# Another order of units in a fused attention and FFN kernel on one core

## The chip, the core and the metric

The kernel runs on one core of a Trainium2 chip. Its matrix engine (TensorE, PE in the profile; PEld are its weight loads), VectorE (DVE), ScalarE (ACT), GpSimd (POOL) and the queue engine SyncE (SP), which here issues the transfers, each take their own instructions strictly in program order and wait for one another by semaphores. The metric is the device time of one execution in microseconds (us), the median of several runs. The profile's span of one execution is a little shorter than that time.

## What is computed

Attention with a local window of 96 keys and 8 global keys, for 4 batches of 8 heads, 768 positions and 64 channels, followed by a feed-forward layer with a maximum of three products:

```
scores = q @ k.T / 8 - slope[head] * dist          # masked to (0 <= i - j < 96) or (j < 8)
a      = softmax(scores)
x      = concat_heads(a @ v)                       # 3072 tokens x 512
h      = max(x @ w1, x @ w2, x @ w3)               # 512 -> 768
out    = h @ w_out                                 # 768 -> 512, float32
```

Inputs and output are float32; the kernel multiplies in bfloat16 and accumulates in float32. The window lets each tile of 128 tokens attend only to itself and the tile before it, whose first 8 key columns and v rows are overwritten with the global ones.

## The kernel before

The program is a list of small units. A string names them in order, and each engine gets its instructions in that order. A unit is a letter, then indices, then often a digit that chooses the engine (0 ScalarE, 1 VectorE, 2 GpSimd; 3 and 4 other ways). The start of the string and the places that the change touches most (cuts marked):

```
SCHEDULE = """
    K0 K1 K2 K3 K4 K5 l1.0 l1.1 D0.3 c0.0.2 B0.1 B1.1 B2.1 B3.0 K6 B4.1 B5.1 c0.1.1 c1.0.2 x0.0.4 B6.1
    B7.1 x0.1.4 S0.0.1 v0 l2.0 l2.1 K7 S0.1.1 G0.0 S1.0.1 S1.1.0 x1.0.3 c1.1.2 M0.0 M0.1 M1.0 v1 x1.1.4
    C0.1.2 v2 A0.1 G1.2 S2.0.1 M1.1 c2.0.2 x2.0.1 C1.1.1 S2.1.0 G2.2 S3.0.1 M2.0 M2.1 C2.1.1 T0.1 S3.1.1
    M3.0 M3.1 c2.1.2 v3 A1.0 C3.1.0 w0.0 V1.2 x2.1.2 w1.0 A2.1 V2.2 A3.0 T1.0 T2.1 T3.1 W1.0.1 W0.0.0
    G3.2 S4.0.0 S4.1.0 F0.0.0 F0.1.0 M4.0 F0.2.0 F0.3.0 G4.1 S5.0.0 M4.1 S5.1.0 w0.1 W0.1.1 w0.2 W0.2.2
    ...
    F6.2.1 F6.1.2 F6.3.1 F6.4.1 F6.2.2 F6.3.2 F6.5.0 F6.4.2 F6.5.1 F6.5.2 E
"""
```

The letters: `l`, `L` load q and k (`l` several tiles at once), `v` loads v, `w` and `o` load weights; `c`, `C`, `W`, `Q` cast what was loaded to bfloat16; `x`, `X` transpose q and k; `K`, `B` make the masks; `S` scores and their exp, `M` the mask, `A` the product with v and the division, `T` the transpose of its result, `G`, `V` copy the global rows; `F c.f.j` is the product of FFN chunk c, 128 columns f, with weight j, `O` the output product of one tile, `E` the last ones, `D` matmuls of zeros. A chunk is 4, 2, 2, 4, 4, 4, 4 tiles in turn. The first six tiles are read by `l` in pairs, then tiles 6 to 9 and 10, 11; later tiles one by one. PSUM has 3 slots for `psH`, one for `psT` and two for scores.

The units of which the prediction speaks, at the lines of the profile (L239 x, L261 X, L283 and L275 S, L288 its exp, L307 M, L322 and L325 A, L349 T, L361 F, L376 O, L427 W, L436 D):

```python
def u_x(n, s, how):
    bb, t0, sz, a, j0, jn = part(n, s)
    dst = batch_T(bb)[:, a, j0:j0 + jn, t0 * 128:(t0 + sz) * 128].rearrange("c j (i e) -> c j i e", e=sz)
    if how >= 4 and jn > 1:
        m = jn // 2
        halves = [(0, m, psT, "tp", nc.scalar.copy), (m, jn, psH, "h", nc.vector.tensor_copy)]
    else:
        pool, tag = (psH, "h") if how in (2, 3) else (psT, "tp")
        halves = [(0, jn, pool, tag, copies[how % 2])]
    tps = [pool.tile([128, sz, hi - lo, 128], BF16, name="tpp", tag=tag) for lo, hi, pool, tag, copy in halves]
    for (lo, hi, pool, tag, copy), tp in zip(halves, tps):
        for e in range(sz):
            for j in range(lo, hi):
                nc.tensor.transpose(tp[:, e, j - lo],
                                    qb["p", n, s][:, e, 2 * j:2 * j + 2].rearrange("i h d -> i (h d)"), identb)
    for (lo, hi, pool, tag, copy), tp in zip(halves, tps):
        copy(dst[:, lo:hi], tp.rearrange("c e j i -> c j i e"))

def u_X(T, how):
    pt = batch_T(T // NT)
    t = T % NT
    qk = pt[:, :, :, 128 * t:128 * t + 128]
    if how == 4:
        nc.sync.dma_start_transpose(out=qk.rearrange("p a j s -> p (a j) s"),
                                    in_=qb[T].rearrange("p a c -> p (a c)"))
        return
    if how == 3:
        tps = [psT.tile([128, NP, 128], BF16, name="tp", tag="tp"),
               psH.tile([128, NP, 128], BF16, name="tpk", tag="h")]
    else:
        tp = psT.tile([128, 2, NP, 128], BF16, name="tp", tag="tp")
        tps = [tp[:, a] for a in range(2)]
    for a in range(2):
        for jp in range(NP):
            nc.tensor.transpose(tps[a][:, jp], qb[T][:, a, jp * 128:(jp + 1) * 128], identb)
    if how == 3:
        nc.scalar.copy(qk[:, 0], tps[0])
        nc.vector.tensor_copy(qk[:, 1], tps[1])
    else:
        copies[how](qk, tp)

def u_S(T, g, how):
    b, t = divmod(T, NT)
    sp = psS.tile([128, 2, 2, 2, 128], FP32, name="sp", tag=f"sp{g}")
    n = 2 if t else 1
    if how:
        for hh in range(2):
            nc.tensor.matmul(sp[:, hh, :, 0:n], identb,
                             bias[:, g, hh, :, 0:2] if t else bias[:, g, hh, :, 2:3],
                             start=True, stop=False, skip_group_check=True)
    for ds in range(2 if t else 1):
        for j2 in range(2):
            jp = 2 * g + j2
            for hh in range(2):
                hsl = slice(64 * hh, 64 * hh + 64)
                nc.tensor.matmul(sp[:, hh, j2, ds], qT(T - ds, 1)[hsl, jp], qT(T, 0)[hsl, jp],
                                 start=not how, stop=True, skip_group_check=True)
    P = p_pool.tile([128, 4, 2, 128], BF16, name="P", tag="P")
    Pt[T, g] = P
    masked[T, g] = how
    nc.scalar.activation(P[:, :, 0:n], sp.rearrange("p a b d n -> p (a b) d n")[:, :, 0:n],
                         AF.Exp, bias=0.0, scale=scale)

def u_A(T, how):
    b, t = divmod(T, NT)
    op = psS.tile([128, 2, 512], FP32, name="op", tag=f"sp{how}")
    for g in range(2):
        P = Pt[T, g]
        for j2 in range(2):
            for hh in range(2):
                h = 4 * g + 2 * j2 + hh
                i = 2 * hh + j2
                o = op[:, g, (2 * j2 + hh) * 65:(2 * j2 + hh) * 65 + 65]
                nc.tensor.matmul(o, P[:, i, 0], heads(va[T])[:, h], start=True, stop=(t == 0),
                                 skip_group_check=True)
                if t:
                    nc.tensor.matmul(o, P[:, i, 1], heads(va[T - 1])[:, h], start=False, stop=True,
                                     skip_group_check=True)
    x = xb_pool.tile([128, H, D], BF16, name="xb", tag="xb")
    xb[T] = x
    rz = z_pool.tile([128, 2, 4], FP32, name="rz", tag="rz")
    o4 = op[:, :, 0:260].rearrange("p g (h e) -> p g h e", e=65)
    nc.vector.reciprocal(rz, o4[:, :, :, 64])
    nc.vector.tensor_tensor(out=x.rearrange("p (g h) d -> p g h d", g=2), in0=o4[:, :, :, 0:64],
                            in1=rz[:, :, :, None].to_broadcast([128, 2, 4, D]), op=ALU.mult)

def u_XT(T, how):
    c, i = where[T]
    if i == 0:
        xT[c] = xT_pool.tile([128, NP, len(chunks[c]) * 128], BF16, name="xT", tag="xT")
    if how == 4:
        nc.sync.dma_start_transpose(out=xT[c][:, :, i * 128:(i + 1) * 128],
                                    in_=xb[T].rearrange("p h d -> p (h d)"))
        return
    if early(T):
        tp = psH.tile([128, NP, 128], BF16, name="xtp", tag="h")
    else:
        tp = psT.tile([128, NP, 128], BF16, name="xtp", tag="tp")
    x = xb[T].rearrange("p h d -> p (h d)")
    for jp in range(NP):
        nc.tensor.transpose(tp[:, jp], x[:, jp * 128:(jp + 1) * 128], identb)
    copies[how](xT[c][:, :, i * 128:(i + 1) * 128], tp)

def u_F1(c, f, j):
    W = len(chunks[c]) * 128
    if f == 0 and j == 0:
        ht[c] = ht_pool.tile([128, NF, W], BF16, name="ht", tag="ht")
    ps = psH.tile([128, W], FP32, name="h", tag="h")
    for dm in range(4):
        nc.tensor.matmul(ps, w123[f // 2][:, dm, j, (f % 2) * 128:(f % 2) * 128 + 128],
                         xT[c][:, dm], start=(dm == 0), stop=(dm == 3))
    if j == 0:
        h01 = h01_pool.tile([128, W], BF16, name="h01", tag="h01")
        h01s[c, f] = h01
        nc.scalar.copy(h01, ps)
    elif j == 1:
        nc.vector.tensor_max(h01s[c, f], h01s[c, f], ps)
    else:
        nc.vector.tensor_max(ht[c][:, f], h01s[c, f], ps)

def u_E():
    n = len(chunks[last])
    pos = [psH.tile([128, DM], FP32, name="po", tag="h") for _ in range(2)]
    for tt in range(2):
        f2_mm(pos[tt], last, tt, range(NF - 1))
    for tt in range(2):
        f2_mm(pos[tt], last, tt, [NF - 1])
        f2_out(pos[tt], last, tt, nc.scalar.copy)
    for tt in range(2, n - 1):
        po = psT.tile([128, DM], FP32, name="po", tag="tp")
        f2_mm(po, last, tt, range(NF))
        f2_out(po, last, tt, nc.scalar.copy)
    for lo, hi, copy, dma in ((0, 256, nc.scalar.copy, nc.sync), (256, 384, nc.vector.tensor_copy, nc.sync),
                              (384, 512, nc.scalar.copy, nc.scalar)):
        po = psH.tile([128, hi - lo], FP32, name="po", tag="h")
        f2_mm(po, last, n - 1, range(NF), slice(lo, hi))
        f2_out(po, last, n - 1, copy, slice(lo, hi), dma)

def u_D(i, n):
    wp = psH.tile([128, 512], FP32, name="wp", tag="h")
    for _ in range(n):
        nc.tensor.matmul(wp, zeros[:, 0:128], zeros, start=True, stop=True)
```

Of the kernel before, what the change touches and what calls it, by code (L numbers as in the profile page):

```python
# [25 lines left out]
    K0 K1 K2 K3 K4 K5 l1.0 l1.1 D0.3 c0.0.2 B0.1 B1.1 B2.1 B3.0 K6 B4.1 B5.1 c0.1.1 c1.0.2 x0.0.4 B6.1  # L26
    B7.1 x0.1.4 S0.0.1 v0 l2.0 l2.1 K7 S0.1.1 G0.0 S1.0.1 S1.1.0 x1.0.3 c1.1.2 M0.0 M0.1 M1.0 v1 x1.1.4
    C0.1.2 v2 A0.1 G1.2 S2.0.1 M1.1 c2.0.2 x2.0.1 C1.1.1 S2.1.0 G2.2 S3.0.1 M2.0 M2.1 C2.1.1 T0.1 S3.1.1
    M3.0 M3.1 c2.1.2 v3 A1.0 C3.1.0 w0.0 V1.2 x2.1.2 w1.0 A2.1 V2.2 A3.0 T1.0 T2.1 T3.1 W1.0.1 W0.0.0
    G3.2 S4.0.0 S4.1.0 F0.0.0 F0.1.0 M4.0 F0.2.0 F0.3.0 G4.1 S5.0.0 M4.1 S5.1.0 w0.1 W0.1.1 w0.2 W0.2.2  # L30
    V3.2 F0.0.1 F0.1.1 F0.0.2 F0.1.2 v4 C4.1.0 A4.0 V4.2 w1.1 W1.1.2 W2.0.0 F0.4.0 F0.5.0 M5.0 M5.1 w1.2
    W1.2.2 v5 W2.1.0 T4.0 F0.2.1 F0.3.1 l3.0 l3.2 F0.4.1 l3.1 c3.0.2 c3.2.2 F0.5.1 o2 C5.1.0 A5.1 l3.3
    F0.2.2 Q2.2 F0.3.2 W2.2.0 o0 T5.0 F0.4.2 o1 F0.5.2 x3.0.0 F1.0.0 F1.1.0 c3.1.1 F1.2.0 x3.2.0 Q0.2
    F1.0.1 F1.1.1 F1.2.1 l4.0 l4.1 c3.3.0 F1.0.2 F1.1.2 F1.2.2 x3.1.2 x3.3.1 F1.3.0 F1.4.0 Q1.2 F1.3.1
    S6.0.0 S6.1.0 v6 v7 v8 G6.0 F1.3.2 F1.5.0 v9 c4.0.1 F1.4.1 S7.0.0 S7.1.0 G7.2 v10 M6.0 M6.1 M7.0
    M7.1 O0.0.0 F1.4.2 c4.1.1 C6.1.2 C7.1.2 L12 F1.5.1 S8.0.0 S8.1.0 x4.0.0 O0.1.0 A6.0 x4.1.2 A7.1 V7.2
    F1.5.2 v11 T6.0 O0.2.0 T7.1 G8.2 C8.1.2 S9.0.0 S9.1.0 G9.1 v12 v13 O0.3.0 F2.0.0 F2.1.0 S10.0.0 M8.0
# [23 lines left out]
def kernel(  # L61
# [13 lines left out]
    nc = tc.nc  # L75
# [46 lines left out]
    zeros = persist.tile([128, 512], BF16, name="zeros")  # L122
# [387 lines left out]
```

The softmax here doesn't subtract the row's maximum and nothing guards it: scores larger than these inputs give would overflow.

## Time and profile before

| what | value |
|---|---|
| time, median of 3 | 180.43 us (180.39 to 180.48) |
| span of the profiled execution | 178.5 us |
| h matmuls (L361), records | 491, busy 99.2 us |
| output matmuls (L376), records | 147, busy 33.1 us |
| transposes by DMA | 11 of x, 9 of q and k |
| HBM traffic | 25.17 MB read, 6.29 MB written |

A busy time is the union of the intervals in which an engine worked; shares are of the span. The chain that ended last is followed back from the last instruction to whatever released each step; its rows give start, length and what ran. A few per cent of the matmul records are missing from the trace, so counts of the program are larger. PEclk is the share of the clock that was granted.

### The profile page before, as it was taken

The page shows a single profiled execution, that of the slowest core. Times are in us where ns is not written, and L with a number is a line of the kernel's source. Part 1 is how long each engine was busy: PE and PEld are TensorE (multiplying, and loading weights), DVE is VectorE, ACT ScalarE, POOL GpSimd, SP SyncE. Part 2 cuts the span into 40 slices and gives each one's busy share as a digit, 9 for nine tenths or more (in the row PEclk, how much of TensorE's full clock was granted, in tenths as well). Part 3 has the DMA queues.
Part 4 walks back from the last instruction along what each step waited for, and adds up shares of the span by engine and source line. Part 5 has one row for each costly group of instructions (what it writes and reads, how often), then busy time and mean ns, then how long its engine had stood idle before and what let it go on. Part 6 is the DMA issues. An engine that isn't in the chain of part 4 may idle for free.

```text
span 178.5 us, 3963 instructions
## 1 busy us (share of the span) xinstructions
PE 167.1 (94%) x1529; PEld 95.9 (54%) x1551; DVE 119.1 (67%) x237; ACT 103.2 (58%) x160; POOL 37.4 (21%) x65
## 2 busy tenths in 40 slices
PE   3599799999999999999999999999999999999991
PEld 0455645458866677845555555454454555444451
DVE  4519975977796689748978448978358986137610
ACT  4867898646689958555753936351862543440131
POOL 4255203543343012210006024100020401000000
PEclk9999999999999999999999999999999999999998
DMA  5999999999998899899544999988989664700015
GB/s 139 292 270 243 357 321 383 319 361 356 252 194 229 218 254 227 142 204 234 92 90 122 167 253 231 145 172 152 182 156 300 123 129 147 252 12 4 0 47 190
DMA packets 83587, 35.52 MB, mean 199 GB/s; under 512 B 66160, under 2 KB 78320, under 8 KB 83568
## 3 DMA queue, kind: packets, MB, share of 16 engines
q1 hardware_dynamic: 83424, 35.20, 83.6%
q8 instruction: 12, 0.20, 0.5%
q10 hardware_dynamic: 144, 0.07, 0.1%
q14 instruction: 7, 0.06, 0.1%
HBM read 25.17 MB, written 6.29 MB: 176 GB/s over the span
## 4 chain that ended last, share of the span: by engine, by line
PE 88%; ACT 3%; DVE 2%; POOL 2%; issue 1%; DMA 1%; POOLq 0%; ACTq 0%
PE h L361 53%; PE po L376 16%; PE sp L283 7%; PE op L322 3%; PE op L325 3%; PE tpp L239 3%; PE xtp L349 2%; ACT wmask L300 2%; PE sp L275 2%; DMA out_dram<-ost 1%; DVE qkT L243 1%; DVE xb L332 1%; ACT ost L382 1%; ACT P L288 1%; PE tp L261 1%
## 5 line engine op out<-in xcount | busy, mean ns | idle before, releaser
L361 PE MATMUL h<-xT,w 128*128 128x512 bf16 (+1 forms) x491 | 99.2, 348 | 0.7 <-issue 0.2
L361 PEld LDWEIGHTS <-w 128*128 128x128 bf16 x504 | 47.0, 98 | 40.4 <-ACT w L427 0.2
L288 ACT ACTIVATE P<-sp 128x1024 bf16<-128x1024 f32 (+1 forms) x48 | 43.4, 954 | 20.4 <-PE sp L283 20.2
L368 DVE TENSOR_TENSOR h<-h,h 128x512 bf16<-128x512 bf16 (+1 forms) x42 | 25.2, 609 | 25.6 <-PE h L361 15.5
L366 ACT CAST h<-h 128x512 bf16<-128x512 f32 (+1 forms) x42 | 21.6, 532 | 21.5 <-PE h L361 21.3
L376 PE MATMUL po<-wo,ht 128*128 128x512 bf16 (+2 forms) x147 | 33.1, 362 | 0.5
L370 DVE TENSOR_TENSOR ht<-h,h 128x512 bf16<-128x512 bf16 (+1 forms) x42 | 25.0, 606 | 3.7 <-PE h L361 3.0
L307 DVE TENSOR_TENSOR P<-P,wmask 128x1024 bf16<-128x1024 bf16 x36 | 24.8, 716 | 3.6 <-ACT P L288 3.5
L382 ACT COPY ost<-po 128x512 f32<-128x512 f32 (+2 forms) x20 | 11.2, 564 | 18.4 <-PE po L376 11.2
L376 PEld LDWEIGHTS <-ht 128*128 128x128 bf16 x156 | 14.0, 98 | 13.8
L332 DVE TENSOR_TENSOR xb<-op,rz 128x512 bf16<-128x512 f32 x24 | 16.6, 691 | 0.8
L283 PEld LDWEIGHTS <-qkT 64*128 64x128 bf16 x352 | 10.2, 96 | 10.0 <-issue 8.0
L283 PE MATMUL sp<-qkT 64*128 64x128 bf16 x352 | 15.2, 223 | 0.4 <-DVE xb L332 0.4
L322 PEld LDWEIGHTS <-P 128*128 128x128 bf16 x192 | 12.5, 97 | 2.7 <-ACT P L288 0.2
L221 POOL COPY va<-vaf 8x260 int32<-8x260 int32 x14 | 6.3, 449 | 34.7 <-PE op L325 34.7
L198 POOL CAST qkb<-raw 128x1024 bf16<-128x1024 f32 x7 | 7.2, 1037 | 27.6 <-DMA raw<-in_k_dram 27.6
L322 PE MATMUL op<-va,P 128*128 128x65 bf16 x160 | 12.4, 193 | 0.3 <-ACT va L189 0.2
L239 PE MATMUL tpp<-identb,qkp 128*128 128x128 bf16 x96 | 8.5, 246 | 4.0 <-POOL qkp L183 3.5
L325 PEld LDWEIGHTS <-P 128*128 128x128 bf16 x160 | 10.4, 97 | 1.8 <-issue 0.2
L239 PEld LDWEIGHTS <-qkp 128*128 128x128 bf16 x96 | 7.0, 112 | 5.8 <-POOL qkp L183 4.4
L325 PE MATMUL op<-va,P 128*128 128x65 bf16 x128 | 9.9, 193 | 0.1
L243 ACT COPY qkT<-tpp 128x1024 bf16<-128x1024 bf16 (+1 forms) x9 | 7.9, 873 | 3.4 <-PE tpp L239 3.4
(66 smaller groups left out, 107.7 us busy)
## 6 DMA issues: line engine op xcount, KB each, us to landing
rawv<-in_v_dram SPq DMA_DIRECT2D x24, 256.0 KB, 4.9
out_dram<-ost SPq DMA_DIRECT2D x23, 256.0 KB, 2.3
rawp<-in_q_dram SPq DMA_DIRECT2D x6, 512.0 KB, 7.3
rawp<-in_k_dram SPq DMA_DIRECT2D x6, 512.0 KB, 7.7
wst<-in_moe_w_dram SPq DMA_DIRECT2D x3, 1024.0 KB, 10.3
raw<-in_q_dram SPq DMA_DIRECT2D x12, 256.0 KB, 4.2
raw<-in_k_dram SPq DMA_DIRECT2D x12, 256.0 KB, 4.7
wst<-in_moe_w_dram SPq DMA_DIRECT2D x3, 512.0 KB, 8.6
```

The costliest lines, as they stand in the source:

```text
L239: nc.tensor.transpose(tp[:, e, j - lo], qb["p", n, s][:, e, 2 * j:2 * j + 2].rearrange("i h d -> i (h d)"), identb)
L283: nc.tensor.matmul(sp[:, hh, j2, ds], qT(T - ds, 1)[hsl, jp], qT(T, 0)[hsl, jp], start=not how, stop=True, skip_group_check=True)
L288: nc.scalar.activation(P[:, :, 0:n], sp.rearrange("p a b d n -> p (a b) d n")[:, :, 0:n], AF.Exp, bias=0.0, scale=scale)
L307: nc.vector.tensor_mul(P, P, wmask[:, g, :, 0:2])
L322: nc.tensor.matmul(o, P[:, i, 0], heads(va[T])[:, h], start=True, stop=(t == 0), skip_group_check=True)
L325: nc.tensor.matmul(o, P[:, i, 1], heads(va[T - 1])[:, h], start=False, stop=True, skip_group_check=True)
L332: nc.vector.tensor_tensor(out=x.rearrange("p (g h) d -> p g h d", g=2), in0=o4[:, :, :, 0:64], in1=rz[:, :, :, None].to_broadcast([128, 2, ...
L361: nc.tensor.matmul(ps, w123[f // 2][:, dm, j, (f % 2) * 128:(f % 2) * 128 + 128], xT[c][:, dm], start=(dm == 0), stop=(dm == 3))
L366: nc.scalar.copy(h01, ps)
L368: nc.vector.tensor_max(h01s[c, f], h01s[c, f], ps)
L370: nc.vector.tensor_max(ht[c][:, f], h01s[c, f], ps)
L376: nc.tensor.matmul(po, ht[c][:, f, tt * 128:(tt + 1) * 128], wo[:, f, cols], start=(f == 0), stop=(f == NF - 1))
```

## The change

The whole list is put into another order. v of tiles 1 and 2 is loaded ahead of the third pair's q and k, and the three first weight blocks w0.0, w0.1, w0.2 ahead of the larger w1.0. The masks that are needed later are made later. The unit of zeros has 54 matmuls of 128 columns instead of 3 of 512; they keep TensorE at work from the start until the first data are there. The transposes of x for tiles 6 to 9 and of q and k for tiles 12, 16 and 18 go from TensorE to DMA, which takes work from TensorE and copies from VectorE and ScalarE. Many casts and small copies move to another engine. A unit of 9 short matmuls of zeros stands after the last unit. What is computed stays the same.

The diff, cut to the head, the places of the moved transposes and the end:

```diff
 SCHEDULE = """
-    K0 K1 K2 K3 K4 K5 l1.0 l1.1 D0.3 c0.0.2 B0.1 B1.1 B2.1 B3.0 K6 B4.1 B5.1 c0.1.1 c1.0.2 x0.0.4 B6.1
-    B7.1 x0.1.4 S0.0.1 v0 l2.0 l2.1 K7 S0.1.1 G0.0 S1.0.1 S1.1.0 x1.0.3 c1.1.2 M0.0 M0.1 M1.0 v1 x1.1.4
-    C0.1.2 v2 A0.1 G1.2 S2.0.1 M1.1 c2.0.2 x2.0.1 C1.1.1 S2.1.0 G2.2 S3.0.1 M2.0 M2.1 C2.1.1 T0.1 S3.1.1
-    M3.0 M3.1 c2.1.2 v3 A1.0 C3.1.0 w0.0 V1.2 x2.1.2 w1.0 A2.1 V2.2 A3.0 T1.0 T2.1 T3.1 W1.0.1 W0.0.0
-    G3.2 S4.0.0 S4.1.0 F0.0.0 F0.1.0 M4.0 F0.2.0 F0.3.0 G4.1 S5.0.0 M4.1 S5.1.0 w0.1 W0.1.1 w0.2 W0.2.2
-    V3.2 F0.0.1 F0.1.1 F0.0.2 F0.1.2 v4 C4.1.0 A4.0 V4.2 w1.1 W1.1.2 W2.0.0 F0.4.0 F0.5.0 M5.0 M5.1 w1.2
-    ... (cut)
-    F1.5.2 v11 T6.0 O0.2.0 T7.1 G8.2 C8.1.2 S9.0.0 S9.1.0 G9.1 v12 v13 O0.3.0 F2.0.0 F2.1.0 S10.0.0 M8.0
-    ... (cut)
-    A9.1 X12.1 M10.0 M10.1 C10.1.0 C11.1.0 F2.2.0 S11.0.0 S11.1.0 M11.0 M11.1 L15 F2.3.0 F2.4.0 O1.1.0
-    V9.2 A10.1 F2.2.1 V10.2 T8.0 F2.3.1 F2.5.0 T9.0 A11.1 F2.4.1 T10.0 F2.2.2 F2.3.2 T11.1 F2.4.2
-    ... (cut)
-    V14.2 F3.3.2 F3.4.2 T13.4 F3.5.2 C16.1.0 C16.0.2 X16.3 T14.4 C17.0.2 A15.1 X17.4 O2.1.0 S16.0.0
-    ... (cut)
-    A16.1 F4.2.0 F4.3.0 S17.0.0 S17.1.0 F4.2.1 F4.0.2 F4.3.1 v18 M17.0 v19 M17.1 X18.3 X19.4 C20.0.0
-    ... (cut)
-    A23.1 T23.4 O5.0.1 O5.1.0 O5.2.1 O5.3.0 F6.0.0 F6.1.0 F6.0.1 F6.0.2 F6.2.0 F6.3.0 F6.4.0 F6.1.1
-    F6.2.1 F6.1.2 F6.3.1 F6.4.1 F6.2.2 F6.3.2 F6.5.0 F6.4.2 F6.5.1 F6.5.2 E
+    B6.1 K5 B5.1 D0.54 l1.0 K6 c1.0.2 B4.1 B0.1 B2.1 K0 B3.0 B7.1 B1.1 c0.1.1 c0.0.0 x0.0.3 K4 x0.1.4 K7
+    S0.1.1 S0.0.1 l1.1 c1.1.1 G0.0 S1.1.0 v0 C0.1.1 S1.0.1 G1.1 x1.0.3 M0.1 M0.0 x1.1.4 A0.1 M1.0 v1 v2
+    S2.0.1 S2.1.0 G2.2 M1.1 S3.0.1 S3.1.1 C1.1.1 C2.1.2 M2.0 M2.1 l2.1 c2.1.1 A1.0 V1.2 K1 x2.1.4 v3
+    T0.1 C3.1.2 A2.1 V2.0 l2.0 c2.0.0 G3.0 w0.0 T1.0 A3.0 x2.0.4 M3.0 w0.1 T2.0 T3.1 w0.2 W0.0.2 W0.2.1
+    W0.1.2 S4.0.0 S4.1.0 M4.1 G4.0 F0.0.0 F0.1.0 F0.1.1 K2 F0.0.1 S5.0.0 S5.1.0 V3.2 w1.0 W1.0.1 F0.0.2
+    K3 M5.0 F0.1.2 F0.3.0 M4.0 F0.2.0 w1.1 W1.1.1 W2.0.2 F0.5.0 F0.4.0 W2.1.2 F0.5.1 v4 C4.1.2 A4.0
+    F0.4.1 M5.1 F0.3.1 w1.2 W2.2.0 W1.2.2 T4.1 V4.2 F0.2.1 M3.1 F0.5.2 v5 C5.1.0 A5.0 l3.1 c3.1.2 F0.3.2
+    F0.2.2 T5.1 l3.0 c3.0.0 x3.1.3 F0.4.2 F1.0.0 F1.4.0 x3.0.4 F1.0.1 F1.0.2 l3.2 c3.2.2 x3.2.3 l3.3
+    ... (cut)
+    v9 Q1.2 G8.1 l4.0 F1.3.2 M7.1 F1.5.1 F1.5.2 O0.2.0 M8.1 A6.1 T6.4 v10 A7.0 V7.2 T7.4 F1.4.2 L12 M8.0
+    O0.0.0 S9.1.0 S9.0.0 c4.1.2 x4.1.4 O0.3.0 M9.1 c4.0.2 M9.0 L13 O0.1.0 L14 x4.0.4 C8.1.2 A8.1 F2.0.0
+    F2.1.0 C11.1.0 F2.3.0 C10.1.1 T8.4 G9.2 S10.0.0 S10.1.0 C9.1.2 F2.1.1 V8.1 F2.0.1 F2.1.2 A9.0 V9.2
+    ... (cut)
+    F2.2.1 V10.0 T9.4 F2.5.0 A11.1 F2.4.0 C13.0.2 X13.4 F2.2.2 T10.1 v13 X12.4 F2.5.1 G12.2 C14.0.2
+    ... (cut)
+    C18.1.2 T13.4 F3.5.1 T14.4 F3.5.2 C16.0.0 S15.1.0 M15.1 S15.0.0 X16.4 X18.4 G15.1 V14.1 L19 O3.2.1
+    ... (cut)
+    O5.0.0 O4.3.0 O5.2.0 F6.0.0 F6.4.0 F6.4.1 O5.3.1 F6.2.0 F6.2.1 O5.1.1 F6.2.2 F6.4.2 F6.0.1 F6.0.2
+    F6.3.0 F6.3.1 F6.3.2 F6.5.0 F6.1.0 F6.1.1 F6.1.2 F6.5.1 F6.5.2 E D1.9
 """
 ...
         for _ in range(n):
-            nc.tensor.matmul(wp, zeros[:, 0:128], zeros, start=True, stop=True)
+            nc.tensor.matmul(wp[:, 0:128], zeros[:, 0:128], zeros[:, 0:128], start=True, stop=True)
```

## The prediction

> **What bounds the kernel now.** I read the page's busy times and slices first, then the chain that ended last in order of time, then the waits, the two phases as windows, and last the DMA issues of the first 22 us one by one.
>
> The page, and of the chain in order of time the rows around the place where the character of the chain changes:
>
> ```profile
> PE 167.1 (94%) x1529; PEld 95.9 (54%) x1551; DVE 119.1 (67%) x237; ACT 103.2 (58%) x160; POOL 37.4 (21%) x65
> PE 88%; ACT 3%; DVE 2%; POOL 2%; issue 1%; DMA 1%; POOLq 0%; ACTq 0%
> ```
>
> ```profile
> 7.69 1.01 PE tpp L239 x8
> ...
> 10.32 0.97 PE sp L275 x2
> ...
> 13.26 1.82 DVE qkT L243 x2
> ...
> 17.57 0.51 PE sp L275 x2
> ...
> 41.04 0.45 PE tpp L239 x8
> ...
> 100.28 3.45 PE h L361 x16
> ...
> 169.63 2.39 PE po L376 x11
> 172.04 0.22 ACT ost L382
> ```
>
> After the first FFN matmul (h, L361, at 23.27 us) the chain is TensorE almost without a break until 172.04 us. Before that it passes from engine to engine, and after it there are 6.4 us of copying out and landing. So the span is three pieces: head 23.3, a stretch of 148.7 that TensorE fills, tail 6.5 (178.5 together; the timed 180.43 has 1.9 more, which I leave as it is).
>
> Is the stretch truly full? The same question as windows (busy PE, count, share of clock):
>
> ```profile
> 0.00:6.20 6.20, 1.48 (x4) 0.30 (x5) 2.81 (x18) 3.93 (x8) 3.23 (x13) 1.00 0.71 182
> 6.20:13.00 6.80, 6.33 (x54) 3.90 (x55) 2.52 (x5) 4.75 (x11) 2.85 (x4) 1.00 1.23 278
> 13.00:23.30 10.30, 8.97 (x154) 6.27 (x152) 9.32 (x18) 8.46 (x11) 3.18 (x6) 1.00 1.18 305
> 23.30:54.00 30.70, 30.49 (x282) 19.31 (x285) 23.58 (x42) 22.22 (x35) 11.14 (x13) 1.00 1.07 311
> ```
>
> A busy TensorE in this profile is no proof, as ends are modelled; so I counted. From the chain: 16 matmuls of 512 columns in 3.45 us are 0.216 each; 12 of 256 in 1.31 are 0.109; 8 transposes in 0.45 are 0.056; 16 score matmuls in 0.55 are 0.034; the op ones follow at 0.03. The program's order has behind the first h: 498 of 512 columns (360 h, 138 po), 150 of 256, 12 narrow po, 280 scores, 296 op and 108 transposes. 107.6 + 16.4 + 0.7 + 9.6 + 8.9 + 6.0 = 149.2; of it 6 wide, 6 half and 12 narrow po (2.6) lie behind 172.04. So 146.6 of 148.7 us is plain throughput, and the rest has to cover 19 changes from full-height to 64-row score matmuls and back. The list of waits gives TensorE 0.2 us of idle there. No wait is left to remove from this stretch; only work can be.
>
> The head hangs on transfers. The DMA issues in order (start, length of the issue):
>
> ```profile
> 6.71 1.74 SPq L158 DMA_DIRECT2D rawp<-in_q_dram  x1
> 8.49 1.66 SPq L158 DMA_DIRECT2D rawp<-in_k_dram  x1
> 10.19 4.84 SPq L174 DMA_DIRECT2D rawv<-in_v_dram  x3
> 15.08 3.74 SPq L417 DMA_DIRECT2D wst<-in_moe_w_dram  x4
> ```
>
> The first weight block (w0.0) is issued at 15.08 and takes 6.2 us to land: 21.2. The last v of the first four tiles is issued at about 13.2 and takes 6.6: 19.8. Behind them
>
> ```profile
> 22.07 1.05 ACT L427 CAST w<-wst 128x1024 bf16<-128x1024 f32 x1
> 22.35 0.40 PE L349 MATMUL xtp<-identb,xb 128*128 128x128 bf16 x4 [0.58 <-DVE xb L332]
> ```
>
> the cast of w0.0 ends at 23.12 and the xT of the fourth tile at 23.2; h starts at 23.27. The attention chain and the weights arrive together.
>
> **The skill.** (1) "TensorE: Matmul & The Clock Gate", Part 1, says that the array's clock is halved until about 3.4 us of sustained activity, and halved again after an idle window. The trace agrees: 8 transposes take 1.01 us at 7.69 but 0.45 at 41.04; two 512-column bias matmuls take 0.97 at 10.32 but 0.51 at 17.57. The granted share (PEclk) shows full clock throughout and hides this. (2) Same page, "Back-to-back issue gap": N/2.4 + 2.5 ns when warm, 216 ns for 512 columns and 56 for 128; the chain shows 216 and 56. The page's lower sustained figure of 131 ns for 512 columns is not seen here. (3) "DMA: Bandwidth & Descriptors", "Queues, rings and completion order": on each DMA engine one queue's descriptors are taken in ring order. The loads here land in the order of issue, so what is issued earlier lands earlier only at the cost of what it overtakes, and a DMA transpose stands behind the loads issued before it.
>
> **The change part by part.**
>
> *Transposes.* T6 to T9 go from TensorE to DMA (16 transposes), and so do X12, X16 and X18 (24). 40 × 0.056 = 2.24 us leave the full stretch. Their PSUM copies (T: 0.42 on VectorE or 0.59 on ScalarE; X: 0.42 + 0.59, or 0.68) go too, but those engines have slack at 67 and 58%. Matmul counts are otherwise equal, as are the 19 changes to score matmuls. On the path: −2.24.
>
> *Zeros.* Three matmuls of 512 columns (0.43 apart when cold) become 54 of 128. At the cold 0.107 each that is 5.8 us from 1.19, so they end between 6 and 7, wholly or partly warm by then. The first real transposes can come at 6.6: q's cast is now on ScalarE behind three wmask (0.43 each from 3.76) and one bias (0.41), then 1.05 for the cast; before, they came at 6.18. No loss, and the transposes, bias and score matmuls of the first two tiles, some 5 us when cold, halve. But k of the second pair lands at 10.5 (issued at 3.30, 7.2 to land) either way, so most of that becomes idle time.
>
> *Head order.* Ten transfers still stand before w0.0, the same ten: it lands near 21.2 as before. v3 moves one place up, ahead of q2, and lands near 17.9 instead of 19.8. The attention chain then is ScalarE's: four exp of the third and fourth tile from about 14.3 (0.97 each) end at 18.2; a wmask (0.43), half of a qkT copy (0.59), a va copy (about 0.3) bring 19.5; the cast of q2, which lands near 19.7, 20.8; then a kg copy (0.22), xT (0.59), half a qkT copy (0.59) and the last xT on ScalarE (0.59): 22.8. The cast of w0.0, now on POOL (1.04), ends at 22.3. So h starts at about 22.9 instead of 23.27: −0.4. The limit is 22.3 whatever else is gained. As much TensorE work lies ahead of the first h as before (48 transposes of q and k, 16 of x, 12 bias, 72 scores, 56 op), so nothing else shifts across that line.
>
> *Weights.* w0.1 and w0.2 now pass w1.0: landing near 22.8, 24.3 and 27.1 (estimates: the same four blocks were through at 27.1 before, when the POOL cast of the last began after 6.29 us of waiting, and half-size blocks followed each other at about 1.5). The new order of h uses them so: two j=0 units to 24.6, then j=1, then two scores, then j=2 at 27, then w1.0's units at 28.7. Each cast is done 0.5 to 2 us ahead. 0.
>
> *Tail.* The last step is unchanged; 9 more short zero matmuls after it end before the last output lands (copies at 175.46, landing after). 0.
>
> *New waits.* T6 and T7 by DMA feed F2.0.0. Between T7 and F2.0.0 lie one half-width h unit (0.44), three output tiles (1.3 each), two sets of transposes (0.45 each), scores (0.55) and op (0.5): 6.3 us. The chain is rz and xb (0.9), issue (1.2) and landing (2.4 when nothing is queued), 4.5; but loads are in the queue until about 54.5, as before, and an output with them, so it may come to 6 or 7. The other moved ones have over 5 us. I put +0.4 for all.
>
> Sum: 180.43 − 2.24 − 0.4 + 0.4 = 178.2 us, a ratio of 0.988.
>
> **Rivals.** (a) *The queue becomes the bound.* There are 27 DMA transposes instead of 20, each 1.2 us of issue on the one in-order queue, with loads and outputs behind waits of their own. For: the DMA share is 0.89 from 54 to 100 us, and the list of waits has ten SyncE waits for ost of 29.6 us in total. Against: POOL waits 27.6 us for raw loads without TensorE noticing, so loads run well ahead. Two or three such stalls of 1 to 2 us would make 180 to 182. (b) *The head is won by the warm clock.* If the first tiles chain through TensorE alone, 3 us would come off beside the 2.24: 175.2. Against: w0.0 lands at 21.2 and needs its cast, which limits the head's gain to 1 us. (c) *The array goes cold again.* The warm-up ends at 6 to 7, then TensorE waits for casts and ScalarE until 22.9. Before, it was cold and thus busy until 13, and then stayed warm through gaps of up to 0.8. If it drops back before the first h, some 3.4 us of h run at half rate: +1.7, 180. (d) *Copies moved between engines delay a PSUM slot*: there are three psH slots and VectorE now waits for w0.2 (24.3) with P and h maxima behind it; +0.5 to 1.
>
> **Range and chances.** All known gains together are 2.24 + 1.0 = 3.2 us, which gives 177.2; beyond 2% (176.8) nothing in the profile leads, save a w0.0 that lands earlier. Losses are open upward: nearly every unit was moved in one go, and one mistimed wait is 0.5 to 2 us. So 177.0 to 180.6, with 6% for faster by over 2%, 86% within 2%, 8% slower than 184.0.
>
> **What would show it.** Right: transposes 56 ns each from about 7 us on; first h at 22.4 to 23.4; stretch from first h to the first copy of the end near 146.5; PE transposes counted 132 instead of 172; tail 6.4 ± 0.3. Wrong: a TensorE wait of over 0.5 us at F2.0.0 or at any h or score behind a DMA transpose (rival a); 512-column matmuls 0.43 apart after the first h (c); first h before 22.2 (b).

## The result and the profile after

The changed kernel takes 188.75 us; the kernel before took 180.43 in the same comparison. The ratio is 1.046, interval 1.044 to 1.048: slower, and outside the predicted range of 177.0 to 180.6. Of its four executions three lie at 188.74 to 188.77; the fourth, 193.07, ran at a lower mean granted clock (0.972 against 0.991 to 0.999), and such executions are left out of all ratios and times below, though the traces read for four runs are of one (the seven transposes back on TensorE, the new head, both queue edits together, the filler).

The span of the profiled execution grew by 8.5 us, from 178.5 to 187.0. The page of the changed kernel, busy times, granted clock in 40 slices, and the chain that ended last by engine:

```profile
PE 169.2 (91%) x1550; PEld 99.1 (53%) x1571; DVE 126.0 (67%) x241; ACT 96.9 (52%) x155; POOL 37.9 (20%) x62
PEclk9997899999999999999999999999999999999999
...
PE 46%; DMA 19%; DVE 18%; issue 7%; SPq 4%; ACT 3%; POOL 1%; ACTq 0%; DVEq 0%; POOLq 0%
```

Before, the chain was 88% TensorE and 1% transfers. Now it is 46% TensorE, 19% transfers and 18% VectorE. The granted clock dips once, to half from 16.80 to 20.21 us. (The record counts of TensorE can't be set against each other, because each trace lacks some records.) The chain in order of time, changed kernel, shows where it leaves TensorE after the first h:

```profile
19.07 0.85 PE tpp L239 x8
...
58.99 4.33 DMA xT<-xb
...
113.39 6.53 DMA qkT<-qkb
119.97 0.62 PE sp L283 x16
...
134.35 5.39 DMA qkT<-qkb
139.79 0.62 PE sp L283 x16
...
168.80 8.37 PE h L361 x38
...
179.62 0.18 ACT ost L382
```

Of the six transfers in it between the first h and the last copies, four are DMA transposes, three of them shown; the other two, a load of k and an output, lead up to the one at 113.39. The list of waits of TensorE in the changed kernel (total, number, longest) says the same; in the list of the kernel before neither line existed:

```profile
PE sp L283 <- DMA qkT<-qkb: 4.9, 4, 1.9
PE h L361 <- DMA xT<-xb: 1.4, 2, 0.8
```

I divided the span as the prediction did:

| piece | before | after | difference |
|---|---|---|---|
| head, to the first h | 23.27 | 24.11 | +0.84 |
| first h to the first copy of the end | 148.77 | 155.51 | +6.74 |
| tail | 6.46 | 7.38 | +0.92 |

For the middle piece I added up every gap between two matmuls that is longer than their own rate (0.216, 0.109, 0.056, 0.034 and 0.03 us by shape). After the first h these gaps sum to 9.0 us: 5.55 at scores that needed q and k from a DMA transpose, 1.6 at h units that needed x from one, and 1.9 behind VectorE work. Before they summed to 0.2. With the 2.24 us of removed transposes that makes −2.24 + 9.0 − 0.2 = +6.6, against +6.74 measured.

The same in windows of the changed kernel (length, then busy PE; the last three columns are the granted clock, the DMA share and GB/s):

```profile
13.00:24.10 11.10, 9.05 (x137) 6.37 (x134) 8.96 (x18) 8.56 (x14) 3.37 (x6) 0.85 1.01 274
62.00:108.00 46.00, 41.72 (x423) 25.39 (x427) 31.93 (x66) 24.68 (x40) 9.08 (x13) 1.00 1.15 206
108.00:142.00 34.00, 30.68 (x272) 15.51 (x276) 23.02 (x40) 19.98 (x32) 4.88 (x8) 1.00 1.07 209
142.00:179.60 37.60, 37.34 (x226) 17.88 (x229) 21.56 (x36) 9.64 (x16) 1.00 (x2) 1.00 0.26 76
```

And of the kernel before:

```profile
62.00:107.00 45.00, 44.47 (x461) 27.13 (x467) 32.79 (x67) 27.55 (x45) 8.67 (x14) 1.00 0.92 179
107.00:142.00 35.00, 34.74 (x271) 17.26 (x274) 25.87 (x48) 18.23 (x26) 5.74 (x10) 1.00 0.91 182
```

TensorE now idles 4.3 us between 62 and 108 and 3.3 between 108 and 142, at a DMA share that the profile gives as over 1; before, it idled 0.5 and 0.3 in the matching windows, at 0.92 and 0.91. From 142 on, when the last loads are through, it is full again.

**One late transpose, step by step.** One of the two longest waits is S22, the scores of tile 22. First the last cast that its transpose needs, then SyncE's queue, then the score matmuls, from the timelines of ScalarE, SyncE and TensorE in the changed kernel (start, length; in brackets the idle time before, and what ended it):

```profile
128.83 1.04 ACT L198 CAST qkb<-raw 128x1024 bf16<-128x1024 f32 x1 [5.07 <-DMA raw<-in_k_dram]
```

```profile
127.91 3.83 SPq L340 DMA_TRANSPOSE xT<-xb  x3
131.79 0.58 SPq L174 DMA_DIRECT2D rawv<-in_v_dram  x1
132.43 0.57 SPq L167 DMA_DIRECT2D raw<-in_q_dram  x1
133.04 1.21 SPq L167 DMA_DIRECT2D raw<-in_k_dram  x1
134.35 2.56 SPq L250 DMA_TRANSPOSE qkT<-qkb  x1
```

```profile
139.79 0.62 PE L283 MATMUL sp<-qkT 64*128 64x128 bf16 x16 [1.84 <-DMA qkT<-qkb]
```

The data are ready at 129.87. But SyncE issues in order. At 129.87 it is still at the three transposes of x (T18, T17, T19), and three loads follow (v21 and the two of L23) before X22 is issued, 4.5 us after its data. With those loads ahead of it on the DMA engines it then takes 5.4 us instead of the 3.1 of the kernel before. TensorE was there at 137.95.

The same reading for every DMA transpose whose room was used up (times in us; room is from landing to first use; taken from the starts and ends in the traces):

| unit | data ready | issued | landed | first use | room after | room before |
|---|---|---|---|---|---|---|
| T7 (new by DMA) | 57.80 | 58.99 | 63.32 | 63.46 | 0.14 | – |
| X14 | 80.52 | 84.48 | 89.57 | 89.71 | 0.14 | 5.45 |
| X15 | 85.49 | 92.39 | 97.09 | 97.14 | 0.05 | 10.87 |
| X16 (new by DMA) | 97.73 | 102.31 | 105.57 | 105.61 | 0.05 | – |
| X19 | 110.86 | 113.39 | 119.92 | 119.97 | 0.05 | 3.67 |
| T19 | 128.30 | 130.53 | 132.94 | 132.99 | 0.04 | 1.32 |
| X22 | 129.87 | 134.35 | 139.74 | 139.79 | 0.05 | 2.07 |

Five of the seven were DMA transposes before, and had room. They weren't moved to DMA; their places in the queue changed, and seven more stand in it. X15 waited longest to be issued, 6.9 us from the end of its cast, behind X14 and five loads.

### The profile page after: what moved, and what is told of

The parts are those of the page before. It is cut to its first block, busy times and chain, and to the rows that moved or that the text cites. A ratio compares the mean times of both kernels' runs of the same rounds, so it can differ in the third digit from the quotient of the medians.

```text
span 187.0 us, 4000 instructions
## 1 busy us (share of the span) xinstructions
PE 169.2 (91%) x1550; PEld 99.1 (53%) x1571; DVE 126.0 (67%) x241; ACT 96.9 (52%) x155; POOL 37.9 (20%) x62
## 4 chain that ended last, share of the span: by engine, by line
PE 46%; DMA 19%; DVE 18%; issue 7%; SPq 4%; ACT 3%; POOL 1%; ACTq 0%; DVEq 0%; POOLq 0%
PE h L361 30%; PE po L376 7%; DMA qkT<-qkb 6%; DVE qkT L243 4%; DMA xT<-xb 4%; PE sp L283 4%; DVE P L307 3%; DMA out_dram<-ost 3%; DVE xb L332 3%; DMA rawp<-in_k_dram 3%; SPq L167 3%; DVE ht L370 3%; DMA raw<-in_k_dram 3%; DVE h L368 2%; ACT P L288 2%
## 5 line engine op out<-in xcount | busy, mean ns | idle before, releaser
L307 DVE TENSOR_TENSOR P<-P,wmask 128x1024 bf16<-128x1024 bf16 x36 | 28.5, 799 | 11.8 <-ACT P L288 11.2
L322 PEld LDWEIGHTS <-P 128*128 128x128 bf16 x192 | 12.7, 99 | 3.0 <-issue 0.5
L322 PE MATMUL op<-va,P 128*128 128x65 bf16 x160 | 13.1, 196 | 0.3 <-DVE P L307 0.3
L198 POOL CAST qkb<-raw 128x1024 bf16<-128x1024 f32 x8 | 8.3, 1038 | 23.3 <-DMA raw<-in_k_dram 23.3
L189 POOL CAST va<-rawv 128x512 bf16<-128x512 f32 x11 | 7.3, 664 | 23.8 <-DMA rawv<-in_v_dram 19.4
L325 PEld LDWEIGHTS <-P 128*128 128x128 bf16 x160 | 10.9, 99 | 1.2
L243 DVE COPY qkT<-tpp 128x512 bf16<-128x512 bf16 (+1 forms) x12 | 10.6, 906 | 0.7 <-PE tpp L239 0.5
L325 PE MATMUL op<-va,P 128*128 128x65 bf16 x128 | 10.0, 193 | 0.3 <-ACT va L221 0.3
L382 DVE COPY ost<-po 128x512 f32<-128x512 f32 (+1 forms) x6 | 3.7, 621 | 7.3 <-PE po L376 5.7
L239 PE MATMUL tpp<-identb,qkp 128*128 128x128 bf16 x96 | 7.6, 227 | 0.6 <-ACT qkp L183 0.3
```

What stands on the lines that cost most here:

```text
L307: nc.vector.tensor_mul(P, P, wmask[:, g, :, 0:2])
```

## The experiments

Theory M: the seven moved transposes cost the time. Theory O: the new order after the first h costs it. Theory H: the new head. Theory Q: the one queue of SyncE, in which a transpose stands behind loads, outputs and other transposes; Q1 is the part of the outputs in it. Theories W and G concern the zeros: the gain of a warm head turns into waits (W), or comes off (G). The text of a run names its own further rivals.

### Undoing or doing one part

**The changed order, its seven moved transposes back on TensorE.**

```diff
-T6.4 T7.4 T8.4 T9.4 X12.4 X16.4 X18.4
+T6.0 T7.1 T8.0 T9.0 X12.1 X16.3 X18.3
```

> The changed order, but T6 to T9, X12, X16 and X18 are done on TensorE with the copies of before. Theory M (the seven moved transposes made the loss, by their waits and by filling the transfer queue): most of the 8.3 us goes, 181 to 183 us. Theory O (the new order made it; only the waits of F2.0.0, 0.94, and S16, 1.93, belong to the moved ones, and 2.24 us of TensorE work come back): 187.5 to 188.5 us, with the waits of S15, S22 and F5.0.0 still there.

Measured 189.7 to 192.0, ratio 1.057 [1.050, 1.064]: slower still. M alone falls: taking the moved transposes back doesn't bring the time back. In this order those transposes stand right behind their producers, so TensorE itself waits for them. Its list of waits:

```profile
PE xtp L349 <- DVE xb L332: 2.2, 2, 1.2
PE tp L261 <- ACT qkT L263: 1.7, 1, 1.7
```

Waits of scores for DMA transposes fall to 0.7 us there, but TensorE also comes to these scores 4 to 7 us later (S15 at 101.3 instead of 97.1), so it can't be told whether the shorter queue or the later TensorE gave them room. A unit's place and its engine belong together: this list was made for transposes by DMA.

**The old order, the same seven by DMA where they stand.**

```diff
-T6.0 T7.1 T8.0 T9.0 X12.1 X16.3 X18.3
+T6.4 T7.4 T8.4 T9.4 X12.4 X16.4 X18.4
```

> The order of before, with T6 to T9, X12, X16 and X18 done by DMA where they stand. Theory M: 184 to 188 us. Theory O: 2.24 us of TensorE work go, some waits of 1 to 2 us come: 178.5 to 181.5 us.

Measured 185.27, ratio 1.027 [1.022, 1.031]. That lies in M's range: in the old order the seven transposes by DMA are enough to lose, so O alone falls too. List of waits of TensorE:

```profile
PE h L361 <- DMA xT<-xb: 2.0, 1, 2.0
PE sp L283 <- DMA qkT<-qkb: 1.3, 1, 1.3
```

F2.0.0 waited 2.2 us for T7, which landed at 62.05 and was used at 62.19; right behind it, from 63.15 on, the array ran at half clock for 3.41 us. F3.0.0 waited 1.35 for T9 (landed at 79.75, used at 79.88), S16 1.3 for X16, and S11 0.45. The three late transposes (T7, T9, X16) are all moved ones. The sum: −2.24, waits +5.3, half clock up to +1.7, less 0.2 of waits that were there before: +4.6, against +4.85 measured.

**The new head, the old order behind it.** All units ahead of F0.0.0 from the new list (w0.0, w0.1, w0.2, then w1.0), the others in the old order.

```diff
-K0 K1 K2 ... w0.0 V1.2 x2.1.2 w1.0 ... S4.1.0 F0.0.0 F0.1.0 M4.0 F0.2.0 ...
+B6.1 K5 B5.1 D0.54 ... w0.0 ... w0.1 ... w0.2 ... G4.0 K2 K3 M3.1 w1.0 W1.0.1 F0.0.0 F0.1.0 M4.0 F0.2.0 ...
```

> All units ahead of the first h in the new order (with the 54 zeros), the rest in the order of before. Theory O with the loss behind the first h: the head costs what the trace shows, first h 0.8 us later, 181 to 181.8 us. Rival H (the late and partly cold head puts everything behind it out of step): 184 us or more.

Measured 188.2 to 190.4, ratio 1.048 [1.039, 1.057], but it tells H and O not apart. The old order of h uses w1.0 third, the new head loads it fourth. F0.2.0 waits 3.8 us for its weight, in TensorE's list of waits:

```profile
PE h L361 <- DVE w L427: 3.7, 1, 3.7
```

This wait, one of 2.8 at F0.5.1, and two stretches at half clock (6.83 and 3.41 us) are of the graft and in neither kernel.

**The old head, the new order behind it.**

```diff
-B6.1 K5 B5.1 D0.54 ... G4.0 F0.0.0 F0.1.0 F0.1.1 K2 F0.0.1 ...
+K0 K1 K2 ... D0.3 ... w1.0 ... G3.2 S4.0.0 S4.1.0 w0.1 w0.2 ... G4.0 F0.0.0 F0.1.0 F0.1.1 F0.0.1 ...
```

> All units ahead of the first h as before (three wide matmuls of zeros), the rest in the new order with its DMA transposes. Theory O with the loss behind the first h: 187 to 188.5 us. Rival H: below 183 us.

Measured 187.9, ratio 1.040 [1.036, 1.045]. 1.9 of it is again a graft (F0.1.1 waits for w0.1, which is loaded behind w1.0). Without that some 5.6 us are lost behind the first h: O as to the place, with the waits at S15 (1.06), S16 (0.78), F4.4.0 (1.7), F5.0.0 (0.7) and S22 (0.6). The one at F4.4.0 is not for a transpose: VectorE waited 3.6 us for an output to land before it could free the slot. The waits are partly others than in the changed kernel; which transfer comes late changes with small shifts.

### The zeros

**54 short zeros in the old order**

```diff
-D0.3       nc.tensor.matmul(wp, zeros[:, 0:128], zeros, ...)
+D0.54      nc.tensor.matmul(wp[:, 0:128], zeros[:, 0:128], zeros[:, 0:128], ...)
```

> The kernel before with 54 matmuls of zeros of 128 columns in place of 3 of 512, nothing else. Theory W (a warm array helps only until the next load, as w0.0 lands at 21.2 anyway): first h 0 to 0.4 us earlier, 180.0 to 180.6 us. Rival C (the array is warm too early, falls back to half clock in the gaps of 10 to 20 us and runs the fourth tile cold): first h 0.5 to 1.5 us later, 181 to 182 us. Rival G (the head was limited by the cold array): 178 to 179 us.

181.03, ratio 1.003 [1.001, 1.004]: not G. The time is above W's range and inside C's, but the trace shows no half clock in the head, so C is not the reason. The array is warm from 4 us on and stays so, yet the first h comes at 23.5, not earlier than 23.27, and h then waits 0.5 us for a weight: the warm array brought nothing, as in W.

**Three wide zeros in the new order**

```diff
-D0.54
+D0.3
```

> The changed kernel with the three wide matmuls of zeros of before at its head (the nine short ones at the end stay). Theory C (the zeros made the array fall back to half clock at 14 to 22 us): first h at about 23.3 us instead of 24.1, 187.7 to 188.2 us. Rival (the order of the head, not the zeros, makes the first h late): first h at 24 or later, 188.5 to 190 us.

189.09, ratio 1.047 [1.043, 1.050]; the first h at 24.4 at full clock. C falls; the short zeros cost nothing that can be told.

**The new order without the nine zeros of the tail**

```diff
-F6.5.2 E D1.9
+F6.5.2 E
```

> The changed kernel without the nine zero matmuls behind the last unit. Theory (they cost nothing; the tail is longer by 0.9 us for another reason, the last landing): 188.6 to 188.9 us. Rival (they hold up the last copies): tail back to 6.5 us, 187.8 us.

Ratio 1.049 [1.045, 1.053], three executions at 186.64, 188.84 and 188.90: no gain that can be told from such scatter. The nine zeros run from 182.21 to 182.87 in the changed kernel, ahead of the last copy, and hold nothing up. In the trace of this run (the one of 186.64) the array kept its clock in the head, and the first h came at 22.97.

### The queue

**Five late transposes ahead of the loads.** X14, X15, X16, X19 and X22 were put directly behind their casts, the loads L16, L17, L18, L20, L23, v17, v18 behind them; some casts and one copy of global rows moved along.

```diff
-X12.4 F2.5.1 G12.2 C14.0.2 ... v14 X14.4 L16
+X12.4 F2.5.1 C14.0.2 X14.4 G12.2 ... v14 X15.4 L16
-V19.2 v21 L23 F4.4.1 F4.4.2 S20.0.0 M20.0 S20.1.0 G20.0 X22.4
+V19.2 X22.4 v21 L23 F4.4.1 F4.4.2 S20.0.0 M20.0 S20.1.0 G20.0
```

> The changed kernel with its own DMA transposes, but the transposes X14, X15, X16, X19 and X22 stand in the SyncE queue ahead of loads that are not needed yet (L16, L17, L18, L20, L23, v17, v18 come later), and G12 no longer stands ahead of the cast for X14. Theory Q (the waits of S14, S15, S16, S19 and S22, 5.4 us in sum, come from transposes that stand behind early loads in the one queue): these waits fall below 1.5 us in sum, the time to 184 to 185.5 us. Rival D (the DMA engines are simply too busy with 27 transposes, wherever they stand): the waits move to other scores, 187.5 us or more.

Measured 194.77, ratio 1.078 [1.073, 1.083]. The waits aimed at are gone, all five, with 1.1 to 9.1 us of room: X14 lands 3.3 us after issue and 9.3 us earlier than in the changed kernel, X15 after 3.1 and 8.2 earlier, X16 4.3 earlier. For these three Q is right, and rival D, whose time fits, is not borne out: with as many transposes in the queue they land quickly. X19 and X22 landed only 0.8 and 1.4 us earlier; most of their room came from TensorE, which reached S19 and S22 5.2 and 2.5 us later. And the time got worse, 9 us above Q's range. TensorE's and VectorE's lists of waits in this run:

```profile
PE h L361 <- DVE ost L382: 4.3, 1, 4.3
```

```profile
DVE ost L382 <- DMA out_dram<-ost: 7.5, 1, 7.5
```

What was moved back in the queue came late instead. Outputs now stood behind X18, issued at 104.63 when its cast was done, and four loads: the one in question was issued at 109.29 and landed at 113.58. VectorE had no free output buffer for 7.5 us, and F4.4.0 waited 4.3 for the slot that VectorE was to copy out. The array then ran 6.83 us at half clock. X23 waited for its own, later loads (2.2), X18 cost 1.4.

**Outputs out of the queue.** The 15 outputs that ScalarE copies are issued by ScalarE's own queue; changed order.

```diff
-        f2_out(po, c, tt, copies[how])
+        f2_out(po, c, tt, copies[how], dma=nc.sync if how else nc.scalar)
```

> The changed kernel, but the 15 output transfers whose copy is on ScalarE are issued by ScalarE's own queue, so they no longer stand between transposes and loads in the SyncE queue. Theory Q1 (the loss comes from one in-order queue in which transposes, loads and outputs wait for each other): waits of scores for DMA transposes fall by half or more, 185 to 187 us. Rival (only loads delay the transposes; outputs don't matter): 188 to 189.5 us.

186.48 and 186.93, ratio 1.035 [1.033, 1.037]: 2 us less than the changed kernel, inside Q1's range. S14, S15 and S19 no longer wait; S16 (1.65), S22 (1.75) and F2.0.0 (1.5) still do. The scores' waits fell from 5.55 us to 3.4, less than the half that Q1 asked for. In the trace the stretch behind the first h is 155.5 us as in the changed kernel, because h waited 1.2 for a weight and other waits grew; what came off is 1.25 in the head and 0.6 in the tail. As one execution without the nine zeros took 186.64 too, a gain by the outputs is not shown; that fewer scores wait is.

**Both.** The edits of the last two runs together.

> The kernel with the transposes ahead of the loads, which took 194.8 us because VectorE waited 7.5 us for an output buffer whose transfers stood behind X17 in the SyncE queue (TensorE: 4.4 us at F4.0.2, then 6.8 us at half clock); here the outputs copied by ScalarE go by ScalarE's queue. Theory Q1: that wait and the half clock behind it vanish, 184.5 to 187.5 us. Rival (the wait has another cause, the load of the seventeenth tile itself): 192 us or more.

192.1 to 194.9, ratio 1.074 [1.069, 1.079]. The wait for the output buffer is gone as expected (it was at F4.4.0 and behind X18, not at F4.0.2 and behind X17, as I had read it), the time isn't: it fits the rival, though not by the cause that the rival named. TensorE's list of waits:

```profile
PE sp L283 <- DMA qkT<-qkb: 4.3, 3, 3.6
PE h L361 <- DMA xT<-xb: 3.9, 3, 2.1
```

S23 waits 3.7 and F2.0.0 2.3: the waits had moved once more. By rearranging alone I didn't find room for 27 transposes.

**Is it the half clock?** In the old order with its seven by DMA, 40 short zeros keep the array busy ahead of F2.0.0.

```diff
-O0.3.0 F2.0.0
+O0.3.0 D2.40 F2.0.0
```

> The order of before with the seven moved DMA transposes (185.3 us), and 40 short zero matmuls (2.2 us of TensorE at full clock) just ahead of F2.0.0, where TensorE waited 2.18 us for T7 and then ran 3.4 us at half clock. Theory H (a wait of some 2 us costs again by the half clock behind it): the filler fills the wait and the clock stays, 183.3 to 184.2 us. Rival (the clock has nothing to do with the wait): 185 to 187.5 us.

184.67, 185.18 and 186.91, ratio 1.025 [1.024, 1.027], where it was 1.027 without them: no gain that can be told. In the one trace F2.0.0 was followed by no half clock, but F3.0.0 and S16 were, by 3.41 us each (after waits of 2.3 and 2.5). The run without the filler says more: one of its executions had full clock from end to end (mean 1.000) and took 185.15 us, two with a mean of 0.988 took 185.14 and 185.38. So the half clock doesn't decide the time, although the sum above seemed to need it.

### Leaving transposes out

These runs leave work out, so that the cost of waiting for a transpose can be measured against not having it. The matmuls stay the same in number and shape.

**The changed kernel without its 12 DMA transposes of q and k.** The scores of tiles 12 to 23 read q and k of the second batch; those transposes and the copies of global keys into them are left out.

```diff
+    NO_X = [12, ..., 23]
     def u_X(T, how):
+        if T in NO_X: return
     # reads: qkT[b] -> qkT[1] for T in NO_X
```

> The changed kernel without its 12 DMA transposes of q and k (and the small global-row copies into their results): the scores of tiles 12 to 23 read the transposed q and k of the second batch, which are long there. It leaves that part of the computation out. Theory Q2 (the waits of S14, S15, S16, S19, S21 and S22, 5.5 us in the trace of the changed kernel, are the largest part of the loss): 182 to 184 us, with the waits at F2.0.0 and F5.0.0 left. Rival (other waits take their place because VectorE and ScalarE are late anyway): 186 us or more.

182.02, ratio 1.010 [1.008, 1.011]: 6.7 us less than the changed kernel, as Q2 said. The window from 108 to 142 of this run:

```profile
108.00:142.00 34.00, 34.00 (x299) 17.00 (x298) 24.39 (x43) 21.34 (x30) 4.78 (x6) 1.00 0.71 152
```

TensorE has no gap left there; after 72 us no wait is over 0.12. But not all 6.7 are the transposes'. From trace to trace the stretch shrank by 4.4 (155.5 to 151.1), the head by 1.2 (first h at 22.95, full clock) and the tail by 1.1; no transpose of q and k by DMA runs in those two. And in the stretch other waits grew: 5.55 us went, but F2.0.0 now waited 1.6 and F0.3.0 0.65 for a weight.

**Also without its 15 DMA transposes of x.** The h of chunks 2 to 6 read the x of the first chunk.

> As the run without the transposes of q and k, and without the 15 DMA transposes of x too: h of the third chunk on reads the first chunk's x, which stays in its own buffer. Both are left out of the computation. Theory Q2: what stays is 180.43 - 2.24 for TensorE, + 0.84 for the head, + 1.9 of waits on VectorE, + 0.9 in the tail: 181 to 182.5 us. Rival: 185 us or more.

182.19, ratio 1.012 [1.009, 1.014]: nothing more comes off. F2.0.0's wait for T7 is gone, and in its place TensorE waits for VectorE, 1.4 at A10 and 0.7 at F2.2.0:

```profile
PE op L329 <- DVE P L314: 1.2, 1, 1.2
```

VectorE was the next to be waited for. (The lines are numbered anew in this kernel; L329 is the op matmul.)

**The control: the old kernel without its 20.** All of its DMA transposes of q, k and x are left out in the same way.

> The control: the kernel before with its 20 DMA transposes left out in the same way (those on TensorE stay). TensorE waits for none of them there, so both theories say 180 to 180.6 us; a lower time would mean that transposes cost even where nothing waits for them.

180.45, ratio 1.000 [0.9995, 1.0011]. In the old order, where they have room, 20 transposes by DMA cost nothing; in the changed kernel the stretch is 4.4 us longer with 12 of them than without.

### A version that beats both

From the old order, only such transposes as have room there, each directly behind its producer.

**Three.** T8 behind A8, T9 and X12 behind A9.

```diff
-A8.0 C12.0.1 ... A9.1 X12.1 M10.0 ... T8.0 F2.3.1 F2.5.0 T9.0
+A8.0 T8.4 C12.0.1 ... A9.1 T9.4 X12.4 M10.0 ... F2.3.1 F2.5.0
```

> The kernel before with only those transposes moved to DMA that have room there: X12 (4.3 us of slack in the run with all seven), and T8 and T9 put directly behind A8 and A9, so that they land by about 70 us for their first use at 75. If distance is what decides, 16 transposes of 0.056 come off: 179.4 to 179.7 us. If any DMA transpose more upsets the queue: 181 us or more.

Two groups of times: 179.80 to 180.07 in nine executions, 181.18 to 181.81 in thirteen; ratio 1.003 [1.001, 1.005]. In the trace, of the quicker group, X12 is ready at 65.53, is issued at 70.65 behind T9, lands at 74.22 and is used at 74.28.

**Two.** X12 stays on TensorE.

```diff
-A8.0 C12.0.1 ... A9.1 X12.1 M10.0 ... T8.0 F2.3.1 F2.5.0 T9.0
+A8.0 T8.4 C12.0.1 ... A9.1 T9.4 X12.1 M10.0 ... F2.3.1 F2.5.0
```

> The kernel before with T8 and T9 alone moved to DMA, directly behind A8 and A9 (slack 3 to 4 us in the run that had X12 moved as well, where X12 was what arrived just in time). 8 transposes of 0.056 come off: 179.9 to 180.1 us in every run, without the second group of runs at 181.5. If the second group comes from any transpose added to the queue: 180 and 181.5 again.

179.88, ratio 0.997 [0.996, 0.998], all eight executions within 0.3 us. Eight transposes of 0.056 are 0.45; the stretch went from 148.77 to 148.33, the time by 0.5. T8 lands with 4.1 us of room, T9 with 3.0.

**Three, with X12 first.**

```diff
-A8.0 T8.4 C12.0.1 ... A9.1 T9.4 X12.4 M10.0
+A8.0 T8.4 C12.0.1 X12.4 ... A9.1 T9.4 M10.0
```

> The kernel before with T8, T9 and X12 by DMA, as in the run with two groups of times, but X12 stands directly behind its cast, ahead of the output and of T9 in the SyncE queue. There X12 was issued 5.1 us after its cast and landed just in time. Theory (the place in the queue decides): X12 is issued within 2 us of its cast, and 16 transposes of 0.056 come off in every run: 179.4 to 179.6 us. Rival (a third transposition in that stretch is too much wherever it stands): some or all runs at 181 or more.

179.87, ratio 0.997 [0.996, 0.998], six executions within 0.15 us. The slower group is gone: X12 is issued at 68.49, lands at 71.56 and has 2.5 us of room, so here the place in the queue decides. But the time is above the 179.4 to 179.6 expected: X12's own 0.45 didn't come off. TensorE's timeline shows why:

```profile
67.04 0.40 PE L283 MATMUL sp<-qkT 64*128 64x128 bf16 x8 [0.27 <-DVE xb L332]
```

The second half of S11 waits for the score slot that A9 used until VectorE had read it. X12's transposes had filled that time; removed, they leave it empty. This and the run before are the best of all, 0.5 us under the kernel before.

## Why the prediction was wrong

**Right.** TensorE is the bound of the middle stretch. The removed transposes are worth 2.24 us there: −2.24 with the measured gaps gives the stretch to 0.15 us. The nine zeros of the tail cost nothing. The head gains little: in seven traces that have this head at full clock throughout, the first h came at 22.86 to 23.62, predicted 22.9. F2.0.0 was named as the likeliest new wait, and T7 did land at first use.

**The step that failed is "New waits": "The other moved ones have over 5 us. I put +0.4 for all."** Measured: 9.0 us. It went wrong in three ways.

- I looked at the moved transposes alone. X14, X15, X19, X22 and T19, which were DMA transposes before, lost 1.3 to 10.8 us of room, since the new order put them behind loads and other transposes. Of the moved ones two came late, T7 (0.9) and X16 (1.9, one of those to which I gave over 5).
- I counted issue from the moment the data are ready, and 2.4 us of landing "when nothing is queued"; I raised both only for T7. In the changed kernel the late ones are issued up to 6.9 us after their data and land 2.4 to 6.5 us after that.
- The sum had nothing for VectorE: rival (d) put waits for its slots at 0.5 to 1 us, but 1.9 of the gaps are waits for it (F0.5.0, F1.4.0, S7, O0.2.0, A10), and leaving all DMA transposes out brought 1.4 us of that kind at A10.

**Rival (a) was the right mechanism, dismissed by a wrong argument.** "POOL waits 27.6 us for raw loads without TensorE noticing, so loads run well ahead." That shows room for the loads. It says nothing of the transposes behind them in the same queue. And its size, two or three stalls of 1 to 2 us, was too small: the waits for transposes alone come to 7.2 us, four of 0.85 to 1.9 and four of 0.2 to 0.7. What it is made of is known in part: without the 12 transposes of q and k the stretch loses 4.4 us, and three of them land 4 to 9 us earlier when they stand ahead of the loads. How much is due to the seven that were added to the queue, and how much to the new places of the others, the runs don't separate.

**Rival (c) came, in the head as I had said, but no h ran at half rate.** The array fell to half clock from 16.80 to 20.21 us (the chain's 0.85 us for 8 transposes at 19.07, the 0.85 of granted clock in the window from 13 on). First h 24.11 instead of about 23.0: +1.1, I had said +1.7 for h itself. It isn't always so: three wide zeros gave 24.4 at full clock, so the order of the head can cost the same without it. And one of the three executions kept its clock (mean 0.999 instead of 0.991) and took the same 188.74 us, so the dip doesn't explain the loss. Rival (b), a head won by the warm clock, did not come.

**Weights, "0".** In the changed kernel no h waited for a weight. Where the first h came at 22.95, F0.3.0 waited 0.65 for one (and h 1.2 where it came at 22.86), so the margins of 0.5 us were as thin as I had read them, and part of the head's gain would have been given back.

**Tail.** I said 0, it is +0.92. All of it lies in the landing of the last output, 2.5 us after issue instead of 1.6. It took 2.25 without the zeros too, and the whole tail was 6.3 with them in the run without q and k transposes, so it isn't they; the cause stays open.

**The chances.** 8% for slower was far too little. Nearly every unit had a new place, and I had worked out room for a handful of transposes.

**Open.** Why the two groups of times exist in the run with three early transposes is only argued from X12's room of 0.06 us. Which of VectorE's works should have stood elsewhere wasn't tried. What the half clock costs where nothing else changes isn't measured.

## What to carry to other kernels

Work taken off a full engine pays only if what replaces it has room, and here that was settled by its place in an in-order queue: list data ready, issue, landing and first use for every transfer of the new order, unmoved ones too, before believing the removed time. Move such work one piece at a time, directly behind its producer; here two pieces brought what they were worth, and seven at once in a new order cost 8 us. An idle slot that a removed piece filled can remain, so that removing it brings nothing.

## What was not expected of the hardware

- A DMA transpose landed later where loads stood ahead of it: after 3.1 us (128 by 1024) and 2.4 (128 by 512) with little queued, after up to 6.5 and 5.5 behind loads. The view of transfers, DMA issues of the changed kernel (number, median us to landing; before it was 2.4 and 3.3):

```profile
xT<-xb SPq DMA_TRANSPOSE x15, 2.8
qkT<-qkb SPq DMA_TRANSPOSE x12, 4.5
```

- The stretches at half clock that end before the record does are 3.41 or 6.83 us long in every trace. The Trainium skill, "TensorE: Matmul & The Clock Gate", Part 1, gives a free-running window of 3413 ns, which agrees. Its table "Why this matters for your kernels" asks for idle gaps of no more than about 3 us; here a wait of 2.2 us was followed by a half-clock stretch (F2.0.0 in the old order with seven by DMA), and so was one of 1.7 (X18 put back on TensorE), so the measurement is stricter. Others were not: S16 and S22 in the changed kernel waited 1.9 each and kept their clock.
- The traces show why. Within a trace all starts of half clock, that at the end of the work included, lie whole multiples of 3.413 us apart (16.80 and 187.46 in the changed kernel, 50 of them; 63.15 and 182.61 in the old order with seven by DMA, 35), and the moment at which the array gets warm in the head lies on the same grid (6.6 us in the changed kernel, 4.0 in the old order with 54 zeros). I added up TensorE's idle time in these windows, every gap above 0.03 us beyond the matmuls' own rate, from 10 us on in the 18 traces that have a half-clock stretch. Of 888 windows at full clock, 17 held 2.17 us or more, and half clock followed each of them; the others held at most 1.95, and it followed none. So the sum over a window counts here, not one wait, and where the windows fall differs from execution to execution. This was read from the traces afterwards; no run was made to test it.
